# A Nyström attention and gated feed-forward kernel: every stage cut into one step per engine, w_out read by fours, and a new written order of 1,091 steps

## The chip, the cores and the metric

The kernel runs on one core of a Trainium2 chip. A core has five engines that run side by side and meet at semaphores: TensorE (PE in the profile; its weight loads are shown apart as PEld), VectorE (DVE), ScalarE (ACT), GpSimd (POOL) and SyncE (SP, which here only issues DMAs). Each engine works through its own instructions strictly in the order in which the program wrote them. The metric is the device time of one execution in microseconds.

## The reference, cut to what matters

Eight batches of eight heads, 576 tokens, 64 numbers per head. Each head goes through a Nyström attention with 32 landmarks (means of 18 tokens), and the result through a feed-forward block without a nonlinearity but with a product in the middle.

```python
q_lm = q.reshape(B, H, 32, 18, D).mean(axis=3)      # and k_lm alike
A  = softmax(q    @ k_lm.T / 8)                     # 576 x 32
Bm = softmax(q_lm @ k_lm.T / 8)                     # 32 x 32
C  = softmax(q_lm @ k.T    / 8)                     # 32 x 576
Z  = Bm.T / (norm1(Bm) * norminf(Bm) + 1e-6)
for _ in range(6):
    Z = 2 * Z - Z @ Bm @ Z                          # inverse of Bm, by iteration
x  = (A @ Z @ C @ v)                                # 8 x 8 x 576 x 64 -> 4608 x 512
out = (((x @ w1) * (x @ w2)) @ w3) @ w_out          # 512 -> 1024 -> 1024 -> 512
```

## The kernel before

**The fold.** As nothing stands between `w3` and `w_out`, the kernel first forms `w34 = w3 @ w_out` once (1024 x 512). Both factors are split into a high and a low fp16 part, and three products are added up (`product`, L526 to L533: 8 row blocks j of 8 chunks c of 3 matmuls of 512 columns, 192 matmuls). TensorE needs `w3` transposed: 64 fp32 transposes of 128x128 through the identity, four to a PSUM tile (`turn` in `fold`, L514 to L523), and ScalarE and VectorE then cut that tile into its two parts (L522, L523). `split` (L508) does the same for `w_out`. Twelve matmuls on zeros (L599) come ahead of it.

**The attention of one batch.** `turn` (L140) transposes q and k in 32x32 blocks on VectorE; `landmarks` adds up the groups of 18 (on GpSimd for all batches but the first); `scores_b`, `norms`, `squares` and six steps of `inverse` (L388) make the inverse of the 32x32 matrices, for two batches at a time in `CHAINS`; `scores_c`, `scores_a`, `values`, `denominators`, `normalise`, `landmark_values` do the rest. Their matmuls use 32-row or 64-row tiles of the array. Landmark queries and keys lie in a tile `lm` in which neighbouring landmarks stand 16 bytes apart (`lmk`, L234), and this view is the stationary operand of L274 and L322, and both operands of L248.

**The feed-forward.** `project` (L430) makes w1 and w2 as the landmarks see them (four parts G0 to G3 per batch), `up` (L451) the two products of 576 tokens for one of eight blocks of 128 features (ScalarE copies the first, L459; VectorE multiplies it with the second, L461), and `down` (L470) the 36 output tiles of 128 tokens: eight matmuls of 512 columns, a copy on ScalarE (L499), two DMAs from SyncE (L502).

**Memory that sets waits.** PSUM has three tiles `big`, one `small`, one `acc` (L89 to L97). `acc` is that of `product` and of `down`. SBUF holds three rows of `w3`, six of `w_out`, four turned halves of `w3`, and q and k of two batches.

**What sets the order.** A string `ORDER` (L32) of words, one for each stage: `U3a.2` is the first half of `up` for block 3 of batch 2, `W0.14` the first half of output tile 14, `F` the next piece of the fold, `TK`, `TQ` the block transposes of k and q, `SK`, `SQ` their landmark sums, `LK`, `LQ`, `LV` the loads. The loop at L656 calls the stage, which writes all of its instructions, for all engines, at that place. So two stages can't be interleaved on one engine in another order than on the others.

Of the kernel before, what the change touches and what calls it, by code (L numbers as in the profile page):

```python
# [29 lines left out]
CHAINS = ((0,), (1, 2), (3, 4), (5, 6), (7,))  # L30

ORDER = """  # L32
F F F F F F F F F F F F F TK0.0 F F F F F TQ0.0 TQ1.0 F F L3.3 F TK1.0 F F F F F SK0.0 SK1.0 F F
SQ0.0 P.4 F F F F L3.5 F L3.7 F F TQ0.1 TK0.1 SQ1.0 F F L3.6 TK1.1 F E.0 F B.0 F C0.0 SK0.1 N.0
F F F A0.0 R.0 FV.0 TQ1.1 F SK1.1 F I0.0 F F D.0 I1.0 F I2.0 Y0.0 Y1.0 SQ0.1 Y2.0 LK0.2 F X.0 F
I3.0 LK1.2 F F F I4.0 V0.0 V1.0 SQ1.1 LQ0.2 LQ1.2 E.1 F LK0.3 TK0.2 TK1.2 F LK1.3 I5.0 F V2.0
LV0.2 F TQ0.2 TQ1.2 A0.1 Z.0 SK0.2 LV0.1 LV1.1 F M0.0 LV2.1 F LV3.1 D.1 Y0.1 Y1.1 Y2.1 G0.0 G1.0
G2.0 M1.0 SK1.2 F SQ0.2 TK0.3 G3.0 TK1.3 C0.1 X.1 F F F F U0a.0 U0b.0 U1a.0 U1b.0 U2a.0 U2b.0
LQ0.3 TQ0.3 LQ1.3 LK0.4 U3a.0 LV1.2 V0.1 U3b.0 SQ1.2 E.2 U4a.0 U4b.0 B.1 U5a.0 U5b.0 N.1 V1.1
SK0.3 V2.1 R.1 U6a.0 U6b.0 TQ1.3 U7a.0 I0.1 M0.1 LK1.4 LQ0.4 U7b.0 W0.0 SK1.3 I1.1 W1.0 I2.1  # L40
A0.2 LV2.2 TK0.4 LV3.2 W0.1 I3.1 TK1.4 W1.1 I4.1 M1.1 LQ1.4 W0.2 TQ0.4 I5.1 W1.2 SQ0.3 SQ1.3
TQ1.4 Z.1 SK0.4 E.3 SK1.4 SQ0.4 LV0.3 C0.2 G0.1 D.2 G1.1 G2.1 W0.3 Y0.2 G3.1 V0.2 V1.2 Y1.2 V2.2
LV0.4 Y2.2 U0a.1 U0b.1 LV1.3 LK0.5 U1a.1 U1b.1 LV1.4 LK1.5 X.2 U2a.1 U2b.1 U3a.1 U3b.1 Z.2 SQ1.4
E.4 U4a.1 U4b.1 U5a.1 G0.2 TK0.5 U5b.1 U6a.1 U6b.1 M0.2 LQ0.5 LQ1.5 W1.3 U7a.1 LV2.3 U7b.1 LV3.3
M1.2 W0.4 G1.2 G2.2 G3.2 B.3 TK1.5 W1.4 U0a.2 A0.3 W0.5 U0b.2 U1a.2 LV2.4 D.3 Y0.3 Y1.3 SK0.5
U1b.2 Y2.3 C0.3 W1.5 LK0.6 U2a.2 U2b.2 U3a.2 W0.6 X.3 U3b.2 U4a.2 N.3 SK1.5 V0.3 V1.3 V2.3 R.3
U4b.2 TK0.6 W1.6 LV3.4 U5a.2 U5b.2 W0.7 TQ0.5 U6a.2 I0.3 M0.3 LK1.6 TQ1.5 W1.7 I1.3 SQ0.5 LQ0.6
U6b.2 W0.8 I2.3 W1.8 I3.3 U7a.2 U7b.2 W0.9 I4.3 M1.3 W1.9 I5.3 A0.4 LQ1.6 Z.3 C0.4 W0.10 G0.3
G1.3 G2.3 D.4 W1.10 Y0.4 LV0.5 SQ1.5 G3.3 E.5 LV1.5 U0a.3 U0b.3 Y1.4 W0.11 TK1.6 Y2.4 U1a.3
U1b.3 U2a.3 U2b.3 LK0.7 X.4 TK0.7 W1.11 TQ0.6 U3a.3 U3b.3 U4a.3 V0.4 V1.4 V2.4 SK0.6 SK1.6 A0.5  # L50
TQ1.6 W0.12 U4b.3 LV2.5 U5a.3 LV3.5 LK1.7 SQ0.6 U5b.3 Z.4 U6a.3 U6b.3 LV0.6 LV1.6 U7a.3 U7b.3
W1.12 M0.4 M1.4 G0.4 W0.13 SQ1.6 E.6 TK1.7 G1.4 G2.4 G3.4 SK0.7 W1.13 D.5 Y0.5 LQ0.7 Y1.5 Y2.5
C0.5 U0a.4 X.5 W0.14 SK1.7 W1.14 U0b.4 U1a.4 U1b.4 B.5 V0.5 V1.5 V2.5 U2a.4 U2b.4 N.5 W0.15
U3a.4 U3b.4 W1.15 A0.6 TQ0.7 R.5 M0.5 W0.16 U4a.4 I0.5 U4b.4 U5a.4 I1.5 U5b.4 U6a.4 I2.5 LV0.7
LQ1.7 TQ1.7 SQ0.7 SQ1.7 W1.16 I3.5 U6b.4 U7a.4 I4.5 M1.5 U7b.4 I5.5 LV2.6 LV1.7 LV3.6 W0.17 Z.5
C0.6 E.7 W1.17 D.6 G0.5 G1.5 G2.5 W0.18 Y0.6 Y1.6 G3.5 Y2.6 U0a.5 U0b.5 X.6 W1.18 U1a.5 U1b.5
U2a.5 B.7 V0.6 V1.6 V2.6 U2b.5 U3a.5 N.7 U3b.5 W0.19 U4a.5 U4b.5 U5a.5 U5b.5 Z.6 U6a.5 W1.19
LV2.7 G0.6 G1.6 G2.6 LV3.7 R.7 W0.20 A0.7 I0.7 W1.20 U6b.5 M0.6 M1.6 W0.21 U7a.5 G3.6 D.7 I1.7
U7b.5 W1.21 U0a.6 U0b.6 Y0.7 U1a.6 Y1.7 U1b.6 W0.22 W1.22 C0.7 U2a.6 W0.23 U2b.6 U3a.6 Y2.7
U3b.6 W1.23 V0.7 V1.7 V2.7 X.7 I2.7 U4a.6 W0.24 U4b.6 I3.7 U5a.6 W1.24 I4.7 U5b.6 U6a.6 I5.7  # L60
W0.25 Z.7 U6b.6 W1.25 M0.7 M1.7 G0.7 W0.26 U7a.6 U7b.6 W1.26 G1.7 G2.7 G3.7 W0.27 U0a.7 U0b.7
W1.27 U1a.7 U1b.7 W0.28 U2a.7 U2b.7 W1.28 U3a.7 U3b.7 U4a.7 W0.29 W1.29 U4b.7 U5a.7 U5b.7 W0.30
U6a.7 U6b.7 U7a.7 W1.30 U7b.7 W0.31 W1.31 W0.32 W1.32 W0.33 W1.33 W0.34 W1.34 W0.35 W1.35
# [4 lines left out]
def kernel(  # L68
# [93 lines left out]
    def constants():  # L162

        mask4 = consts.tile([128, 4, 32], FP32, name="mask4")
        eye = consts.tile([128, 2, 32], FP32, name="eye")
        onesq = consts.tile([128, 2, 4, 2, 4], FP16, name="onesq")
        nc.vector.memset(mask4, 0.0)
        nc.vector.memset(onesq, 0.0)
        for h in range(4):
            sl = slice(32 * h, 32 * h + 32)  # L170
            nc.vector.memset(mask4[sl, h, :], 1.0)
            for qd in range(2):
                nc.vector.tensor_copy(out=eye[sl, qd, :], in_=ident[sl, sl])
                nc.vector.memset(onesq[sl, qd, :, qd, h:h + 1], 1.0 / X64)

        selc = consts.tile([128, 2, 4, 128], FP16, name="selc")
        lomask = consts.tile([128, 1], FP32, name="lomask")
        selr = consts.tile([128, 8], FP32, name="selr")
        nc.vector.memset(selc, 0.0)
        nc.vector.tensor_tensor(out=selr, in0=eye[:, 0, 0:8], in1=eye[:, 0, 8:16], op=ALU.add)  # L180
        nc.vector.reduce_sum(out=lomask, in_=eye[:, 0, 8:16], axis=AX.X)
        nc.vector.tensor_scalar(out=lomask, in0=lomask, scalar1=-1.0, scalar2=None, op0=ALU.mult)
        for c in range(4):
            sl = slice(32 * c, 32 * c + 32)
            for qd in range(2):
                nc.vector.tensor_copy(
                    out=selc[sl, qd, c, :].rearrange("p (h m) -> p h m", m=32),
                    in_=selr[sl, 4 * qd:4 * qd + 4].unsqueeze(2).to_broadcast([32, 4, 32]),
                )
        eye2 = consts.tile([128, 32], FP32, name="eye2")  # L190
        nc.vector.tensor_tensor(out=eye2, in0=eye[:, 0], in1=eye[:, 0], op=ALU.add)
        bt = consts.tile([128, 4, 64], FP32, name="bt")
        for i in range(4):
            nc.vector.tensor_copy(out=bt[:, i, 32:64], in_=eye[:, 0])
        xsp = [consts.tile([128, 256], FP32, name=f"xsp{i}") for i in range(2)]
        for t in xsp:
            nc.vector.memset(t, 0.0)
        return mask4, eye, eye2, onesq, selc, lomask, bt, xsp


# [18 lines left out]
    def exchange(st):  # L219
        if st["b"] < 2:  # L220
            psE = big()
            for x in range(2):
                nc.tensor.matmul(psE[:, 0, 256 * x:256 * x + 256], pick[:, x, :],
                                 st["lm"][:, :, x].rearrange("p t l c e -> p t (l c e)"),
                                 start=True, stop=True)
            nc.scalar.copy(out=st["lm"].rearrange("p t x l c e -> p x t (l c e)"),
                           in_=psE[:, 0, :].rearrange("p (x t f) -> p x t f", x=2, t=2))
            return
# [104 lines left out]
    def values(st, n):  # L333
        if n == 0:
            st["psV"] = big()
# [169 lines left out]
    def fold(pf, wof, w3f, wsp, warm_up):  # L505
# [39 lines left out]
        for n, (j, c) in enumerate(order):  # L545
            for f, *args in before.get(n, ()):
                f(*args)
# [158 lines left out]
```

## Time and profile before

| | |
|---|---|
| time, median of 3 runs | 264.17 us (264.1 to 264.42) |
| span of the profiled execution | 261.8 us |
| PE busy | 251.5 us, 96% of the span |
| DVE, ACT, POOL busy | 173.8, 134.7, 103.2 us |
| granted TensorE clock, mean | 0.999 |
| DMA | 37.78 MB, mean 144 GB/s |

No time is given for the profiled execution as a whole; its span, from the first to the last instruction of the program, is 2.4 us below the median of the runs. A line of the groups is read so: line of the code, engine, operation, what it writes and reads, partitions x elements, how many; then busy time, the mean in ns of one, and the idle time of its engine just before them.

### The profile page before, as it was taken

The page shows a single profiled execution, that of the slowest core. Times are in us where ns is not written, and L with a number is a line of the kernel's source. Part 1 is how long each engine was busy: PE and PEld are TensorE (multiplying, and loading weights), DVE is VectorE, ACT ScalarE, POOL GpSimd, SP SyncE. Part 2 cuts the span into 40 slices and gives each one's busy share as a digit, 9 for nine tenths or more (in the row PEclk, how much of TensorE's full clock was granted, in tenths as well). Part 3 has the DMA queues.
Part 4 walks back from the last instruction along what each step waited for, and adds up shares of the span by engine and source line. Part 5 has one row for each costly group of instructions (what it writes and reads, how often), then busy time and mean ns, then how long its engine had stood idle before and what let it go on. Part 6 is the DMA issues. An engine that isn't in the chain of part 4 may idle for free.

```text
span 261.8 us, 10518 instructions
## 1 busy us (share of the span) xinstructions
PE 251.5 (96%) x4578; PEld 148.7 (57%) x4578; DVE 173.8 (66%) x352; ACT 134.7 (51%) x305; POOL 103.2 (39%) x134
## 2 busy tenths in 40 slices
PE   7999999998989999999999999999999999999993
PEld 3455554454556558557654674766476556656642
DVE  8765887556958687788856958767775656464410
ACT  4543236343652565576449546746646555455531
POOL 3630018998981999027092597504400000000000
PEclk9999999999999999999999999999999999999999
DMA  6999998999963448976668496933640713222355
GB/s 236 333 243 284 245 248 191 183 137 240 175 105 50 120 101 167 216 195 114 131 100 162 101 214 150 161 58 86 147 86 3 173 43 80 45 62 61 81 118 127
DMA packets 25070, 37.78 MB, mean 144 GB/s; under 512 B 4672, under 2 KB 13120, under 8 KB 25024
## 3 DMA queue, kind: packets, MB, share of 16 engines
q1 hardware_dynamic: 14704, 24.65, 36.9%
q0 software_dynamic: 9728, 11.54, 28.1%
q10 hardware_dynamic: 592, 0.92, 1.1%
q8 instruction: 36, 0.59, 1.0%
q14 instruction: 10, 0.08, 0.1%
HBM read 38.80 MB, written 9.44 MB: 184 GB/s over the span
## 4 chain that ended last, share of the span: by engine, by line
PE 89%; DVE 4%; ACT 3%; issue 1%; DMA 1%; SPq 0%; DVEq 0%; ACTq 0%
PE big L455 23%; PE acc L495 22%; PE acc L530 14%; PE big L442 5%; PE big L344 5%; PE big L399 4%; PE big L517 2%; PE small L530 2%; PE big L382 2%; PE small L421 2%; PE big L274 1%; PE big L495 1%; PE big L322 1%; DVE ab L461 1%; PE small L248 1%
## 5 line engine op out<-in xcount | busy, mean ns | idle before, releaser
L455 PE MATMUL big<-ahat,gt 128*128 128x288 f16 x512 | 73.1, 287 | 0.7 <-DVE ab L461 0.6
L495 PE MATMUL acc<-w,ab 128*128 128x512 f16 x264 | 67.2, 380 | 0.0
L461 DVE TENSOR_TENSOR ab<-a_sb,big 128x576 f16<-128x576 f16 x64 | 48.0, 750 | 27.2 <-ACT a_sb L459 16.8
L455 PEld LDWEIGHTS <-gt 128*128 128x128 f16 x512 | 48.3, 98 | 21.1 <-issue 3.1
L459 ACT CAST a_sb<-big 128x576 f16<-128x576 f32 x64 | 40.8, 640 | 33.9 <-PE big L455 32.9
L206 POOL TENSOR_TENSOR tr<-qkT 128x1024 f32<-128x1024 f16 x14 | 29.7, 2123 | 70.0 <-DVE qkT L143 69.8
L530 PE MATMUL acc<-wsp,w3t 128*128 128x512 f16 x168 | 41.3, 380 | 0.7 <-ACT w L533 0.5
L495 PEld LDWEIGHTS <-ab 128*128 128x128 f16 x280 | 25.3, 98 | 24.9 <-issue 3.5
L499 ACT ACTIVATE o_sb<-acc 128x512 f32<-128x512 f32 x33 | 19.8, 599 | 19.5 <-PE acc L495 19.1
L530 PEld LDWEIGHTS <-w3t 128*128 128x128 f16 x192 | 18.1, 98 | 18.9 <-issue 1.3
L143 DVE STREAM_TRANSPOSE qkT<-qkn 128x576 uint32<-128x576 uint32 x32 | 24.0, 763 | 2.0 <-DMA qkn<-in_k_dram 2.0
L448 DVE TENSOR_SCALAR gt<-big 128x1024 f16<-128x1024 f32 x16 | 19.1, 1211 | 3.1 <-PE big L442 3.0
L446 ACT ACTIVATE gt<-big 128x1024 f16<-128x1024 f32 x16 | 15.9, 1032 | 5.9 <-PE big L442 5.9
L211 POOL TENSOR_TENSOR tr<-tr 128x512 f32<-128x512 f32 x14 | 17.9, 1282 | 0.6
L442 PE MATMUL big<-wup,zt 64*32 64x512 f16 x512 | 17.4, 380 | 0.2 <-ACT en L282 0.2
L523 DVE SCALAR_TENSOR_TENSOR w3t<-big,w3t 128x512 f16<-128x512 f32 x16 | 11.0, 687 | 10.0 <-ACT w3t L522 10.0
L522 ACT ACTIVATE w3t<-big 128x512 f16<-128x512 f32 x16 | 9.5, 596 | 13.9 <-PE big L517 13.8
L284 DVE STREAM_TRANSPOSE ent<-en 128x576 f32<-128x576 f32 x16 | 12.1, 768 | 4.4 <-ACT en L282 4.4
L344 PE MATMUL big<-vt,ent 64*32 64x64 f32 x1152 | 14.2, 226 | 0.0
L282 ACT ACTIVATE en<-big 128x288 f32<-128x288 f32 x32 | 12.7, 411 | 2.9 <-PE big L274 2.7
L344 PEld LDWEIGHTS big<-vt,ent 64*32 64x32 f32 x1152 | 12.7, 105 | 2.0 <-ACT a_sb L459 0.5
L328 ACT ACTIVATE eat<-big 128x576 f16<-128x576 f32 x16 | 9.6, 652 | 7.3 <-PE big L322 7.3
(214 smaller groups left out, 285.2 us busy)
## 6 DMA issues: line engine op xcount, KB each, us to landing
out_dram<-o_sb SPq DMA_DIRECT2D x70, 128.0 KB, 2.5
vt<-in_v_dram SPq DMA_DIRECT2D x16, 288.0 KB, 5.3
vt<-in_v_dram SPq DMA_DIRECT2D x32, 144.0 KB, 4.0
qkn<-in_k_dram POOLq DMA_DIRECT2D x12, 288.0 KB, 5.4
qkn<-in_q_dram POOLq DMA_DIRECT2D x12, 288.0 KB, 4.9
w3f<-in_moe_w_dram SPq DMA_DIRECT2D x6, 512.0 KB, 6.7
wup<-in_moe_w_dram POOLq DMA_DIRECT2D x4, 512.0 KB, 25.3
wof<-in_moe_w_out_dram SPq DMA_DIRECT2D x6, 256.0 KB, 4.5
```

The lines of the kernel that those rows point to most:

```text
L143: nc.vector.transpose(out=st["qkT"][:, t, prs].rearrange("p c r q e -> p (c r q e)").bitcast(U32), in_=st["qkn"][:, t, prs, :].rearrange(" ...
L206: add(out=tr, in0=x[:, :, 0:4, :], in1=x[:, :, 4:8, :], op=ALU.add)
L211: add(out=tr[:, :, 0:2, :], in0=tr[:, :, 0:2, :], in1=tr[:, :, 2:4, :], op=ALU.add)
L344: nc.tensor.matmul(psV[32 * o:32 * o + 32, qd, 0:64], ent[sl, pr, r, :], vt[sl, pr, 64 * r:64 * r + 64], start=(r == 0), stop=(r == RT - 1 ...
L442: nc.tensor.matmul(psG[o:o + 32, qd, :], zt[rs, i, h, :], wup[rs, h, w, fs], start=(i == 0), stop=(i == 1), tile_position=(64 * qd, o))
L448: nc.vector.tensor_scalar(out=g[:, :, w, fs], in0=psG, scalar1=1.0 / ZS, scalar2=None, op0=ALU.mult)
L455: nc.tensor.matmul(p[:, c, 0:HS], st["g"][:, qd, w, 128 * j:128 * j + 128], st["ahat", qd][:, c, :], start=(qd == 0), stop=(qd == 1))
L459: nc.scalar.copy(out=st["a_sb"], in_=p[:, :, 0:HS])
L461: nc.vector.tensor_tensor(out=st["ab"][:, j, st["t0"]:st["t0"] + S].rearrange("p (c s) -> p c s", c=2), in0=st["a_sb"], in1=p[:, :, 0:HS], ...
L495: nc.tensor.matmul(pso[:, :], ab[:, j, t0:t0 + 128], w34[:, j, :], start=(j == 0), stop=(j == 7))
L499: nc.scalar.activation(out=o_sb, in_=pso, func=AXF.Copy, scale=1.0 / (X64 * X64))
L530: nc.tensor.matmul(psW[j][:, :], turned[j, c // 4][:, a, c % 4, :], wsp[:, b, c, :], start=(c == 0 and a + b == 0), stop=(c == 7 and a == 1))
```

## The change

All stages become generators that yield after what they have for one engine. The order has a word for each such part: `U3.2` appears four times (matmuls, copy, matmuls, product), `W.14` four times (half the matmuls, the other half, copy, DMAs), `I2.3` three times (matmuls, VectorE, ScalarE), and so on; the parts of different stages can be woven in any way that keeps each stage's own order. Written out in parts, the old order has 1,091 as well, and the instructions are the same in number, but for what follows.

- `fold` is gone; `split`, `turned_w3` and `product` are steps of the order, as are the loads of q, k, w1 and w2 at the start, the single warm-up matmuls and eleven pieces of the constants on VectorE.
- The rows of `w_out` are read by fours: chunk c of half x holds rows 512x + 4m + c on partition m, where it was rows 128c + m. To fit, the transposes take every fourth column of a row of `w3`, that is fp32 numbers 16 bytes apart, where they were neighbours. `NPE = 8` makes all of the transposes TensorE's: the branch with a block transpose on VectorE, and the loads cut in eight, are there for j of 8 and more, and there are none.
- The GpSimd copy that holds back the load of row block 4 writes four numbers per partition instead of one.

```diff
-F F F F F F F F F F F F F TK0.0 F F F F F TQ0.0 TQ1.0 F F L3.3 F TK1.0 F F F F F SK0.0 SK1.0 F F
-SQ0.0 P.4 F F F F L3.5 F L3.7 F F TQ0.1 TK0.1 SQ1.0 F F L3.6 TK1.1 F E.0 F B.0 F C0.0 SK0.1 N.0
...
-U3a.4 U3b.4 W1.15 A0.6 TQ0.7 R.5 M0.5 W0.16 U4a.4 I0.5 U4b.4 U5a.4 I1.5 U5b.4 U6a.4 I2.5 LV0.7
-LQ1.7 TQ1.7 SQ0.7 SQ1.7 W1.16 I3.5 U6b.4 U7a.4 I4.5 M1.5 U7b.4 I5.5 LV2.6 LV1.7 LV3.6 W0.17 Z.5
-C0.6 E.7 W1.17 D.6 G0.5 G1.5 G2.5 W0.18 Y0.6 Y1.6 G3.5 Y2.6 U0a.5 U0b.5 X.6 W1.18 U1a.5 U1b.5
...
+NPE = 8
...
+K S.0 K K K K T0.0 K T0.0 K L.2 K S.0 T0.0 S.1 K S.1 K K K T0.1 T0.1 S.2 S.3 LK1.2 KC T0.1 F.0 S.4
+F.0 F.1 S.2 LO.7 KC F.1 LO.6 T1.0 KC F.0 S.3 F.1 L.3 KC T1.0 KC LF F.0 T1.0 F.1 TK1.2 S.5 T1.1 KC
+T1.1 T1.2 S.4 S.5 F.0 S.7 S.6 F.0 T1.1 T0.2 S.6 T1.2 F.1 T0.2 F.0 S.7 T0.3 F.0 F.1 F.0 T0.2 T1.3
+T1.2 LF F.2 F.2 KC TK0.0 F.2 LQ0.2 T1.3 F.2 F.2 F.2 TK1.0 TQ0.0 T1.3 F.2 LK0.2 F.1 P.4 P.4 KC T0.4
...
+R.5 U4.4 LV2.6 U0.4 U4.4 U6.4 U0.4 U4.4 W.15 I0.5 W.16 U6.4 I0.5 I0.5 M0.5 U4.4 I1.5 I1.5 U5.4 LV1.7
+I1.5 TK1.7 I2.5 I2.5 U5.4 W.16 I2.5 I3.5 U7.4 LV3.6 M0.5 I3.5 I3.5 I4.5 I4.5 W.16 SK0.7 I4.5 U6.4
+U6.4 U7.4 I5.5 I5.5 I5.5 W.17 U7.4 U7.4 Z.5 Z.5 C.6 W.17 SK1.7 Z.5 C.6 U5.4 C.6 E.7 U5.4 G0.5 D.6
+C.6 G3.5 W.16 G0.5 W.17 LV2.7 G2.5 G2.5 G3.5 G1.5 G1.5 D.6 W.18 LV1.6 U4.5 U4.5 U0.5 W.17 U0.5 U4.5
...
-        eng.dma_start(out=wof[c], in_=moe_w_out[128 * c:128 * c + 128, :])
+        eng.dma_start(out=wof[c], in_=moe_w_out.rearrange("(x m c) o -> x c m o", x=2, c=4)[c // 4, c % 4])
...
-                nc.tensor.transpose(out=pst[:, 0, 128 * c4:128 * c4 + 128],
-                                    in_=w3f[j][:, 512 * cc + 128 * c4:512 * cc + 128 * c4 + 128],
-                                    identity=ident[:, :])
...
+    def turned_w3(j, cc):
+        if j < NPE:
+            wt = big()[:, 0, :]
+            src = w3f[j].rearrange("p (x m c) -> p x c m", x=2, c=4)
+            for c in range(4):
+                nc.tensor.transpose(out=wt[:, 128 * c:128 * c + 128], in_=src[:, cc, c], identity=ident[:, :])
...
+        yield
+        w3t = w3ts[j, cc] = pf.tile([128, 2, 4, 128], FP16, name="w3t", bufs=4)
+        hi, lo = (w3t[:, i].rearrange("p c j -> p (c j)") for i in range(2))
+        nc.scalar.activation(out=hi, in_=wt, func=AXF.Copy, scale=WS)
+        yield
+        nc.vector.scalar_tensor_tensor(out=lo, in0=wt, scalar=WS, in1=hi,
+                                       op0=ALU.mult, op1=ALU.subtract)
...
-    def up(st, j, w):
...
+    def up(st, j):
+        for w in range(2):
+            p = big()
...
+            yield
+            if w == 0:
+                a_sb = po.tile([128, 2, HS], FP16, name="a_sb", bufs=2)
+                nc.scalar.copy(out=a_sb, in_=p[:, :, 0:HS])
+                yield
...
-        nc.gpsimd.tensor_copy(out=w3f[j][:, 0:1], in_=sts[0]["qkn"][:, 1, 0, 0:1])
+        nc.gpsimd.tensor_copy(out=w3f[j][:, 0:DF:DF // 4],
+                              in_=sts[0]["qkn"][:, 1, 0, 0:1].to_broadcast([128, 4]))
...
+    pab, live = [], {}
     for word in ORDER.split():
...
+        if live[word] is not None:
+            next(live[word], None)
```

In the new order k and q of batch 2 are loaded before those of batch 1 (`LK1.2` ahead of the six steps `LF`, which load k and q of batches 0 and 1 and then w1 and w2), and w1 and w2 after those.

## The prediction

> **What bounds the kernel now.** I read the page first, its busy times and the chain.
>
> ```profile
> PE 251.5 (96%) x4578; PEld 148.7 (57%) x4578; DVE 173.8 (66%) x352; ACT 134.7 (51%) x305; POOL 103.2 (39%) x134
> ...
> PE 89%; DVE 4%; ACT 3%; issue 1%; DMA 1%; SPq 0%; DVEq 0%; ACTq 0%
> ```
>
> TensorE carries 89% of the chain, so a change to the order can win only TensorE's waits. The table of stretches tells how much that is. Its columns are stretch and length, then busy time and instructions of PE, PEld, DVE, ACT and POOL, the granted clock, DMA share and GB/s.
>
> ```profile
> 50.00:60.00 10.00, 8.73 (x240) 5.04 (x237) 4.94 (x11) 3.40 (x8) 9.09 (x12) 1.00 1.01 160
> 70.00:80.00 10.00, 8.41 (x196) 6.12 (x194) 7.09 (x14) 5.05 (x15) 7.79 (x10) 1.00 0.69 107
> 110.00:120.00 10.00, 10.00 (x194) 5.42 (x193) 8.78 (x15) 6.83 (x23) 4.03 (x3) 1.00 0.77 173
> ```
>
> Over all stretches from 6.5 to 250 us PE is idle for 4.6 us: 1.3 in 50 to 60, 1.6 in 70 to 80, 0.5 from 20 to 40, 0.4 from 80 to 100, and from 110 on only 0.3. The waits by engine, for PE, say what ended the larger ones.
>
> ```profile
> PE big L349 <- issue: 1.3, 1, 1.3
> ...
> PE small L290 <- DVE bm L260: 1.0, 1, 1.0
> PE big L455 <- DVE ab L461: 0.6, 2, 0.4
> PE acc L530 <- ACT w L533: 0.5, 2, 0.2
> ```
>
> The 1.3 us of "issue" wait for nothing that a new order promises to mend. So about 3.3 us are to be won from idle time, all of it before 110 us; the second half of the kernel can only lose.
>
> The groups of like instructions, shapes apart, give the price of the transposes that the change alters, and of loads of weights and matmuls with and without a step of 16 bytes:
>
> ```profile
> L517 PE MATMUL big<-ident,w3f 128*128 128x128 f32 x64 | 10.0, 280 | 0.3 <-DMA w3f<-in_moe_w_dram 0.3
> L442 PEld LDWEIGHTS <-zt 64*32 64x32 f16 x512 | 6.0, 91 | 8.7 <-issue 4.1 <-ACT a_sb L459 0.7 <-ACT zt L426 0.2
> L248 PE MATMUL small<-lm 32*32 32x32 f16 x128 | 2.9, 231 | 0.0
> L322 PEld LDWEIGHTS <-lm 32*32 32x32 f16 x256 | 2.5, 134 | 1.9 <-issue 1.9
> L305 PEld LDWEIGHTS small<-bt 32*32 32x32 f32 x128 | 2.1, 105 | 0.8 <-issue 0.4 <-DVE csT L293 0.2
> L399 PE MATMUL big<-sz__1620,tz__1618 32*32 32x32 f32 x32 | 0.4, 197 | 0.0
> ```
>
> And the chain in order of time (start, us, what) shows what a step costs with its neighbours.
>
> ```profile
> 52.36 0.44 PE big L517 x4
> ...
> 85.07 0.38 PE big L399 x32
> 85.45 0.97 PE acc L495 x4
> 86.42 0.38 PE big L399 x32
> ...
> 215.55 0.86 PE acc L495 x4
> ```
>
> Four transposes take 0.44 us (0.11 each). Half an output tile takes 0.86 us, but 0.97 ahead of a step on 32-row tiles: going from the whole array to small tiles costs 0.11.
>
> **The change, part by part.** The sum is made against the profiled span of 261.8 us; the runs' median is 2.4 us above it, and I add the same difference to both.
>
> *Transposes that read every fourth number.* 64 transposes, now with numbers 16 bytes apart. No row has fp32 at that step, but `lm` has fp16 at exactly 16 bytes: a load of 32 such columns takes 134 ns (L322), where 32 fp32 columns side by side take 105 (L305) and 32 fp16 columns 91 (L442). As a moving operand 32 such columns take 231 ns (L248) against 197 for fp32 side by side (L399). So whichever operand is meant, the step costs: 29/32 = 0.9 ns a column from the fp32 load, 34/32 = 1.1 from the matmul, 43/32 = 1.3 from the fp16 load. For 128 columns that is 116, 136 and 172 ns more than 110. The bounds are 0 (the load hidden behind the matmul before it) and 172. I take 116, by the fp32 row, the nearest in type. Eight transposes (row blocks 0 and 1, first halves) lie ahead of 8.9 us, where TensorE waits for VectorE anyway; if that cover is gone, they cost 0.9. The other 56 lie between matmuls of the fold, where PE was busy: 56 x 0.116 = **+6.5** (0 to +9.6).
>
> [...]
>
> *Head.* The constants held VectorE from 0.9 to 6.5 us; the first product came at 6.9 and the first of row block 1 at 8.9. Now the constants are spread out, and w_out's low parts come first. But the second low part of w3 stands behind `KC` (0.7: two memsets and the first masks), so that I add up 6.8 for the first, 7.5 for w_out's second, 8.2, 8.9: the product of row block 1 begins when it did. Then VectorE has three more `KC`, `TK1.2` (0.77) and a fifth ahead of w_out's chunk 4: by the same addition it is ready at 14.9, and PE would be there at 13.6. The 12 transposes between cover 12 x 0.116 = 1.4 of it: **0** (without that cover +0.5 against before, which had waits of its own there).
>
> *Queues.* `LK1.2` goes on GpSimd's queue ahead of the copy that holds back the q and k loads. 288 KB at that queue's price (28.1% of 16 engines for 11.54 MB, so 6.4 us of all engines a MB) is 1.8 us taken from the first loads. The ones pushed back are w_out's chunks 2 to 5 (landed at 7.2 to 8.9) and w3's second halves (8.2, 9.5), used at 9.5 or later: 0, at most +1.8. On SP, row block 2 of w3 moves ahead of the last two w_out chunks, which wait for their buffers: 0, since these landed at 10.9 and 12.3 and are used at about 16. Row blocks 4 and 6 are issued when k of batch 0 has landed (17.6 before) and took 6.4 and 7.6 us to land, so about 25 and 27; PE gets there at 20.7 + 5 + the longer transposes, 27: 0, at most +1. w1 and w2, now behind k and q of three batches, landed at 42.8 and are used at 63.7; with 2.4 MB more ahead, at the 7.5 us a MB at which that queue ran from 9.5 to 42.8, they land at 60: 0. Output DMAs as steps of their own free SP from waiting for copies; no PE wait in the list hangs on SP, 0. Four numbers in the GpSimd copy instead of one: 193 ns (L624) for 183 (L619), 0. w_out by fours: 2 KB a partition as before, 0 to +1.
>
> *Waits that go.* In the fold a row block's copy to `w34` held `acc` twice (0.5); now a transpose or a product of block 1 stands between: **-0.5**. In 70 to 80 us PE waited 1.6, the most of it for `bm` after 24 matmuls; `B.1` and `N.1` now have nine PE steps between them. But by the mean durations VectorE has 11.7 us of work from `G3.0` to `R.1` and PE 11.2, so `big` will still be late by some tenths at a time: **-1.0** (0 to -1.6).
>
> *Switches.* Counted along the written orders, steps on small tiles follow whole-array steps 57 times instead of 65, and are followed by them as often: 8 x (0.11 + 0.09), where 0.09 is what the same chain gives for the way back (a part of `project` takes 0.56 ahead of a whole-array step and 0.47 otherwise): **-1.6** (0 to -1.6).
>
> *Waits that come.* A step of the inverse follows the one before it after VectorE's and ScalarE's parts (292 and 372 ns): from the first's end at 85.4 to the next start at 86.3, 0.92. Before, 0.8 or more of other work lay between. In the new order of batches 5 and 6, `I1`, `I3` and `I4` are followed by one half of `up` only (0.49 + 0.09): 3 x 0.34 = **+1.0** (0 to +1.0). Behind `C.6` stand `G0.5 G3.5 G2.5 G1.5` with three `big` tiles; ScalarE (two exponentials of 1.24, then 1.03) and VectorE (0.77, then 1.21 twice) free them later than PE asks: **+0.6** (0 to +1.5).
>
> Sum: 6.5 - 0.5 - 1.0 - 1.6 + 1.0 + 0.6 = +5.0, a span of 266.8, and 264.2 + 5.0 = **269.2 us**.
>
> **The rivals.**
> *The step costs nothing* (ends on the other side). If the transposes stay at 0.11, the sum is -1.5, and the head's 0.5 is uncovered: -1.0, 263.2. For it: PEld is busy for 57% only and runs beside PE. Against it: four transposes take 0.44 while each of their loads takes 144 ns, so the loads already stand in the pace. It decides at 1.5/56 = 27 ns a transpose. [...]
> *The step costs more*: 172 ns by the fp16 row, 9.6 in all: 272.3.
> *w2 comes late*: if its queue ran at 8.9 us a MB instead of 7.5, w2 would land at 70 and PE would just wait (`G1.0` comes after 56.2 us of PE work; `U0.0`, after 61.7 us of it, started at 69.7, so 8.0 of waits, and 6.5 of longer transposes: 70.7); each us a MB beyond adds 7. I put +3: 272.2. Against it: a reserve of 10 us.
> *The order does what it can and the step is free*: none of the waits that come, -3.1: 261.1.
>
> **How the numbers follow.** Forecast 0.53, step dearer 0.17, w2 late 0.05, step free 0.17, order alone 0.08. 0.2% (0.5 us) is about what runs of this kernel can tell from no change. Slower is 0.53 + 0.17 + 0.05 = 0.75; the free step at 263.2 lies near that bound, so 0.03 of its 0.17 goes to "same", and faster is 0.22. The range from 262.5 to 274 leaves out the order alone and a dearer step with the bounds of the other terms. The likeliest case by itself spans 267 to 271.5.
>
> **What would show it.** The transposes' line: start to start 0.22 to 0.28 where it was 0.11, loads of 230 ns and more, PE's idle time about the same. `U0.0` (69.7 before) starts at 75 to 76. The waits for `bm` and for `w` are gone, and L399 waits for `sz_` about 170 us. The forecast is wrong if the transposes' loads stay near 144 ns, or if `U0.0` starts before 71.

## The result and the profile after

The changed kernel takes 286.44 us (median of 4 runs, 285.11 to 287.14), the kernel before 264.3 beside it: a ratio of 1.082 (95% interval 1.077 to 1.087), 22 us slower. The prediction had the direction, 269.2 us, and a range that ended at 274. The profiled execution has a span of 283.3 us, 21.5 more than before. Times here are medians of a kernel's runs within 1.5% of its fastest, as the ratios are; where that leaves runs out, the median of all follows in brackets.

The page of the changed kernel, lines of its parts 1 to 4 (busy time of each engine, granted clock in 40 slices, the queue that brings instructions, the chain):

```profile
PE 257.3 (91%) x4578; PEld 153.0 (54%) x4578; DVE 173.1 (61%) x352; ACT 132.6 (47%) x305; POOL 103.2 (36%) x134
...
PEclk9999999989995999999999979999999999999998
...
q8 instruction: 36, 0.59, 0.9%
...
PE 69%; DMA 15%; issue 6%; DVE 5%; SPq 3%; ACT 1%; POOL 0%; ACTq 0%; POOLq 0%
```

TensorE's share of the chain fell from 89% to 69%. DMA took 15% of it and "issue" 6%, where each had 1%. Nearly all of the DMA part lies ahead of 54 us, in loads of `w_out` and of k (the last of them from 38.1 to 53.8 us). The clock has dips that it did not have. The table of stretches says where (columns as in the prediction):

```profile
50.00:60.00 10.00, 6.62 (x78) 3.09 (x76) 4.78 (x11) 2.32 (x7) 9.41 (x13) 0.83 1.17 209
70.00:80.00 10.00, 10.00 (x175) 5.71 (x152) 8.07 (x12) 5.82 (x15) 6.92 (x9) 1.00 0.40 90
80.00:90.00 10.00, 6.26 (x184) 4.77 (x183) 4.14 (x12) 3.05 (x12) 9.37 (x12) 0.82 0.96 172
110.00:120.00 10.00, 9.04 (x112) 6.82 (x118) 7.75 (x15) 5.80 (x11) 1.34 (x3) 1.00 0.75 159
160.00:170.00 10.00, 7.27 (x202) 4.53 (x201) 5.21 (x10) 1.69 (x4) 5.53 (x6) 0.83 0.57 158
```

The stretch from 70 to 80 is full, as hoped. Four others now hold 3.4, 3.7, 1.0 and 2.7 us of idle TensorE, and in three of them the clock fell to 0.82 or 0.83. The waits of TensorE name the causes:

```profile
PE big L337 <- issue: 8.5, 3, 3.7
PE big L396 <- ACT sz__694 L409: 3.4, 1, 3.4
PE big L396 <- issue: 2.0, 1, 2.0
PE big L527 <- DMA w3f<-in_moe_w_dram: 1.4, 1, 1.4
PE big L460 <- issue: 1.4, 2, 0.9
...
PE acc L544 <- DVE wsp L519: 1.1, 1, 1.1
PE small L282 <- DVE bm L247: 0.7, 1, 0.7
PE big L396 <- ACT sz__3850 L409: 0.3, 1, 0.3
```

All of TensorE's waits in this view add up to 21.2 us, before to 5.8. "Issue", a wait that nothing in the profile releases, is 8.5 + 2.0 + 1.4 = 11.9 of it, where it was 1.3. Three of these waits stand in the middle of `values` (L337), as the timeline (start, duration, what, idle time before) shows for the largest:

```profile
82.27 0.93 PE L337 MATMUL big<-vt,ent 64*32 64x64 f32 x71
86.95 0.53 PE L337 MATMUL big<-vt,ent 64*32 64x64 f32 x17 [3.74 <-issue]
...
88.16 2.13 PE L460 MATMUL big<-ahat,gt 128*128 128x288 f16 x8
```

One stage stops for 3.7 us between two of its own matmuls, with the same operands ready; behind the wait, eight matmuls of `up` take 2.13 us at a granted clock of 0.50, where eight took 1.14 from 182.8 us at 1.00.

**A theory.** Queue q8 brings instructions: 36 packets of 16 KB in either kernel, and TensorE has some 9,200 records (4578 matmuls, as many weight loads and some 45 waits for semaphores), so 256 to a packet. I counted how many of these had begun when an "issue" wait set in:

| kernel | waits set in at (us) | begun by then | remainder by 256 |
|---|---|---|---|
| before | 58.4 | 1217 | 193 |
| after | 83.0, 111.8, 139.8, 162.3, 216.7, 242.5 | 1985, 3265, 4289, 5313, 7617, 8641 | 193 each time |

And while TensorE waited, or just before, a packet of q8 was on its way. So theory F: TensorE has one block of 256 instructions ahead and no more. When it passes the end of a block the next is asked for; in these two traces 51 of the 72 packets start within 2 us behind that, 7 ahead of it and 14 later (at the latest 4.1), they take 0.9 to 1.8, and TensorE goes on 1.2 to 1.6 us after the end of the one it waited for. A block whose 256 instructions pass in less than all that, some 3.5 us as I estimate it from these numbers, ends in a wait. `values` has 320 instructions in 1.6 us (from 186.2 us in the changed kernel). In the changed kernel the blocks that ended in waits had passed in 1.3 to 3.4 us; in the kernel before, the shortest without one took 3.84 (from 84.5 us), and the one with one 4.2, its packet 3.4 late. Seven packets of these two traces started over 3 us after TensorE had gone on into the next block, all of them while the DMA engines were at a share of 1.0 to 1.2; whether that is what held them back was not tested. The rivals: the neighbourhoods of the new order, the load of v, and the transposes of the prediction.

### The profile page after: what moved, and what is told of

Same layout as the page of the kernel before. It is cut to its first block, busy times and chain, and to the rows that moved or that the text cites. A ratio compares the mean times of both kernels' runs of the same rounds, so it can differ in the third digit from the quotient of the medians.

```text
span 283.3 us, 10482 instructions
## 1 busy us (share of the span) xinstructions
PE 257.3 (91%) x4578; PEld 153.0 (54%) x4578; DVE 173.1 (61%) x352; ACT 132.6 (47%) x305; POOL 103.2 (36%) x134
## 4 chain that ended last, share of the span: by engine, by line
PE 69%; DMA 15%; issue 6%; DVE 5%; SPq 3%; ACT 1%; POOL 0%; ACTq 0%; POOLq 0%
PE big L460 23%; PE acc L502 19%; DMA qkn<-in_k_dram 12%; PE big L445 6%; PE big L337 5%; PE acc L544 4%; PE big L396 4%; DMA wof<-in_moe_w_out_dram 3%; SPq L512 2%; PE big L378 2%; PE small L422 1%; PE big L261 1%; PE big L316 1%; PE small L298 1%; DVE gt L452 1%
## 5 line engine op out<-in xcount | busy, mean ns | idle before, releaser
L460 PE MATMUL big<-ahat,gt 128*128 128x288 f16 x512 | 74.5, 291 | 1.7 <-issue 1.4
L502 PE MATMUL acc<-w,ab 128*128 128x512 f16 x264 | 68.0, 383 | 0.1
L465 ACT CAST a_sb<-big 128x576 f16<-128x576 f32 x64 | 39.9, 641 | 47.8 <-PE big L460 28.9
L460 PEld LDWEIGHTS <-gt 128*128 128x128 f16 x512 | 49.5, 100 | 22.9 <-issue 3.8
L544 PEld LDWEIGHTS <-w3t 128*128 128x128 f16 x192 | 18.8, 100 | 20.7 <-issue 2.8
L337 PE MATMUL big<-vt,ent 64*32 64x64 f32 x1152 | 14.6, 228 | 8.5 <-issue 8.5
L450 ACT ACTIVATE gt<-big 128x1024 f16<-128x1024 f32 x16 | 15.9, 1025 | 6.5 <-PE big L445 6.5
L337 PEld LDWEIGHTS big<-vt,ent 64*32 64x32 f32 x1152 | 12.8, 106 | 10.2 <-issue 9.0
L445 PE MATMUL big<-wup,zt 64*32 64x512 f16 x512 | 18.0, 387 | 0.0
L130 POOL DMA_DIRECT2D qkn<-in_q_dram x14 | 10.2, 733 | 12.4 <-DVE qkT L166 9.3
L382 DVE TENSOR_TENSOR ahat<-eat,big 128x576 f16<-128x576 f16 x16 | 11.8, 748 | 3.4 <-PE big L378 3.4
```

What stands on the lines that cost most here:

```text
L337: nc.tensor.matmul(psV[32 * o:32 * o + 32, qd, 0:64], ent[sl, pr, r, :], vt[sl, pr, 64 * r:64 * r + 64], start=(r == 0), stop=(r == RT - 1 ...
L445: nc.tensor.matmul(psG[o:o + 32, qd, :], zt[rs, i, h, :], wup[rs, h, w, fs], start=(i == 0), stop=(i == 1), tile_position=(64 * qd, o))
L460: nc.tensor.matmul(p[:, c, 0:HS], st["g"][:, qd, w, 128 * j:128 * j + 128], st["ahat", qd][:, c, :], start=(qd == 0), stop=(qd == 1))
L465: nc.scalar.copy(out=a_sb, in_=p[:, :, 0:HS])
L502: nc.tensor.matmul(pso[:, :], ab[:, j, t0:t0 + 128], w34[:, j, :], start=(j == 0), stop=(j == 7))
L544: nc.tensor.matmul(psW, w3ts[j, c // 4][:, a, c % 4, :], wsp[:, b, c, :], start=(c == 0 and a + b == 0), stop=(c == 7 and a == 1))
```

## Experiments

**The order before, its blocks shifted by 120 instructions.**

```diff
-    warm_up(7)
+    warm_up(3)
+    for i in range(64):
+        sl = slice(32 * (i % 4), 32 * (i % 4) + 32)
+        nc.tensor.matmul(psw[sl, 0, 0:32], warm[sl, 0:32], warm[sl, 0:32], start=True, stop=True,
+                         tile_position=(sl.start, sl.start))
```

> The kernel before with its order untouched. Four of the wide warm-up matmuls at the start give way to 64 tiny ones (32x32, 32 columns, on zeros), so that TensorE's stream holds 120 instructions more ahead of all real work; the work and the result are the same. **Theory F (fetch):** TensorE's instructions arrive in blocks of 256, and only one block ahead; a block of which the 256 instructions pass in less than about 3.5 us makes TensorE wait for the next. In the trace of before the ends of the blocks lie so that no block but one passes in under 3.9 us. Moved by 120, eight blocks do (at about 56, 80, 99, 127, 157, 176, 204 and 232 us, each within the 64-row matmuls of `values`), and the sum of what they lack of 3.6 us is 15.6: 277 to 285 us, with 'issue' waits of 1 to 3 us at these places. **Rival (the order):** the waits without a releaser belong to steps that stand beside each other in the new order or to a load; nothing of that is touched here, so 264 to 265 us and 'issue' waits of 1.3 in all, as before.

Measured: 288.6 us, ratio 1.086 (1.079 to 1.094). The old order, shifted, is as slow as the new one. TensorE's waits in this kernel:

```profile
PE big L344 <- issue: 4.6, 3, 1.8
PE small L305 <- issue: 4.4, 2, 2.2
PE big L399 <- issue: 4.0, 2, 2.6
PE big L322 <- issue: 2.9, 1, 2.9
```

15.9 us of "issue"; all eight waits set in with the remainder 193 (1217, 2241, 3265, 4289, 5569, 6337, 7617, 8641). The sum of what the blocks lacked, 15.6, was right; the rest of the 24 is clock (0.967) and some 1.7 us at the head, where four wide warm-ups fewer left TensorE idle before its first transposes.

**The control, 256 instructions more.** One wide warm-up fewer, 129 tiny matmuls.

> The control: the kernel before, its order untouched, with one wide warm-up matmul fewer and 129 tiny ones more, that is 256 instructions of TensorE more ahead of the work. **Theory F (fetch, blocks of 256):** the ends of the blocks fall on the same work as in the kernel before, so the waits go again: 264 to 266.5 us, 'issue' waits of 1 to 2 us in all. **Rival (the tiny matmuls themselves, or any longer stream, cost the time that the shift by 120 showed):** at least the 288 us of that run.

Measured: 264.68 us, ratio 1.002 (0.999 to 1.005). A whole block more costs nothing that the runs show; the waits are those of before:

```profile
PE big L349 <- issue: 1.3, 1, 1.3
...
PE small L290 <- DVE bm L260: 1.0, 1, 1.0
```

Besides them only a wait of 0.9 us in the fold is new. So neither the tiny matmuls nor the longer stream made the loss of the first run, but where the blocks end. This decides for theory F against the neighbours, which are the same in all three kernels.

**The dose, 48 instructions more.** Seven warm-ups, 24 tiny matmuls.

> The kernel before with 24 tiny matmuls more after its seven warm-up matmuls: 48 instructions. **Theory F (fetch):** the sum of what the blocks lack of 3.6 us is 8.0 here, where it was 15.6 for a shift by 120, which cost 24 us; so about +11, 272 to 280 us, with the largest waits about 98 (2.2 us), 199 (2.3) and 155 us (1.0). **Rival (the blocks have another length, or there is slack for more than one of them):** 264 to 266, or as much as the shift by 120.

Measured: 277.37 us, ratio 1.047 (1.041 to 1.052), 10.8 us of "issue", the largest 2.5 us at 100.8, 2.3 at 179.3 and 1.7 at 207.8. The size was forecast from the blocks' durations alone (11 us more, measured 13); the wait at 179.3 was not among those named.

**The changed kernel, shifted by 104.** The same loop with 52 tiny matmuls behind the first five warm-ups.

> The changed kernel with 52 tiny matmuls on zeros (104 instructions of TensorE) after its first five warm-up matmuls, where TensorE waits for w3. **Theory F (fetch):** the waits without a releaser change place. Those at 83 and 162 us (inside `V.1` and `V.3`) go, and 2 to 3.5 us each come at about 62, 107, 184 and 213, with 1 to 3 left at 138 to 142 and at 242. Their sum by the blocks' durations is 13.4 against 9.3 for the changed kernel as it is: 288 to 296 us. **Rival (the order or the load of v):** the waits stay inside the same four steps, at 83, 140, 162 and 242 (plus the cost of the tiny matmuls, under 1): 286 to 287.5 us.

Measured: 289.5 us (289.85), ratio 1.092 (1.086 to 1.099), 15.7 us of "issue". That time alone hardly parts it from the changed kernel (1.077 to 1.087); the places of the waits do. The wait at 162 went; new ones stand at 63.3, 110.2, 185.4 and 215.1, and two are left at 144.6 and 245.7, as forecast. The one at 83 moved to 89.0, into `R.1`, which I had not forecast. All have the remainder 193.

**The fours undone.**

```diff
-        eng.dma_start(out=wof[c], in_=moe_w_out.rearrange("(x m c) o -> x c m o", x=2, c=4)[c // 4, c % 4])
+        eng.dma_start(out=wof[c], in_=moe_w_out[128 * c:128 * c + 128, :])
...
-            src = w3f[j].rearrange("p (x m c) -> p x c m", x=2, c=4)
+            src = w3f[j].rearrange("p (x c m) -> p x c m", x=2, c=4)
```

> The changed kernel with w_out read by rows of 128c + m again, and the transposes taking columns that are neighbours; order and steps as changed. **As predicted (the step of 16 bytes costs 0.116 a transpose):** 6.5 us less, 279 to 281 us. **Rival (the trace of after: start to start 120 ns in the middle where it was 109, so 11 ns for each of 56):** 0.6 us less, 285 to 287 us, and the loads' mean back from 206 to about 144 ns.

Measured: 284.96 us, ratio 1.077 (1.071 to 1.083), which overlaps the interval of the changed kernel: 1.5 us less, and not 6.5. The loads of the transposes, in the groups of the changed kernel and then of this one:

```profile
L527 PE MATMUL big<-ident,w3f 128*128 128x128 f32 x64 | 10.9, 301 | 1.6 <-DMA w3f<-in_moe_w_dram 1.4
L527 PEld LDWEIGHTS big<-ident,w3f 128*128 128x128 f32 x64 | 9.6, 206 | 4.1 <-issue 2.6
```

```profile
L527 PEld LDWEIGHTS big<-ident,w3f 128*128 128x128 f32 x64 | 8.4, 156 | 4.7 <-issue 3.0
```

The step of 16 bytes makes a load 50 ns longer (206 against 156), but the median from start to start only 11 (120 against 109), 0.7 us for 64. In the trace of the changed kernel such loads start 0.12 us apart and last 0.21 each (from 14.9 us), so that they overlap, and most of the longer load does not show in the pace. Nor does the time of the kernel show it: 1.071 to 1.083 here, 1.077 to 1.087 in the changed kernel.

**The turns of k of batch 3 later.** `TK0.3` and `TK1.3` go behind VectorE's part of `I4.0`.

```diff
-... LV3.1 F.5 F.5 TK0.3 A.0 I0.0 I0.0 ... I1.0 I2.0 TK1.3 I2.0 F.6 ... V.0 I4.0 E.1 F.6 D.0 I4.0 V.0 E.1
+... LV3.1 F.5 F.5 A.0 I0.0 I0.0 ... I1.0 I2.0 I2.0 F.6 ... V.0 I4.0 E.1 F.6 D.0 I4.0 TK0.3 TK1.3 V.0 E.1
```

> The changed kernel with the two turns of k of batch 3 on VectorE (`TK0.3`, `TK1.3`) moved behind the fifth inverse step of batch 0, so that VectorE no longer waits for that load between two inverse steps. **Theory W (the late load of k of batch 3 holds VectorE, and so the inverse, and so TensorE):** the wait of 3.4 us at 51.4 goes, and with it the half clock from 55 to 59; -4 to -5 us, 281 to 283 us. **Rival (TensorE would wait there for its next block of instructions or for w3 anyway, or makes the gain up later by a wait for the next block):** -1.5 or less, 285 to 287 us.

Measured: 283.3 us (285.4), ratio 1.076 (1.066 to 1.085), an interval that overlaps that of the changed kernel; two runs took 283.3 us and two 287.5. In the profiled run, one of 287.5, the wait of 3.4 for `sz_` is gone from the list and others have come:

```profile
PE big L396 <- issue: 3.5, 2, 1.9
...
PE big L207 <- POOL lm L200: 0.7, 1, 0.7
```

A block's end at 61 us now costs 1.5, and `E.1` waits for GpSimd's landmark sums; "issue" is 14.2 us in all, where it was 11.9. So the late load makes the wait for `sz_`; whether mending it wins 3 us or nothing, this run does not decide.

**More to do, and faster.** 176 instructions that do nothing, in two places of the changed kernel.

```diff
+PAD = {(0, 1): 64, (3, 1): 24}
...
     def up(st, j):
         for w in range(2):
             p = big()
+            for i in range(PAD.get((st["b"], j), 0) if w == 0 else 0):
+                sl = slice(32 * (i % 4), 32 * (i % 4) + 32)
+                nc.tensor.matmul(p[sl, 0, 0:32], st["g"][sl, 0, 0, 0:32], st["ahat", 0][sl, 0, 0:32],
+                                 start=True, stop=True, tile_position=(sl.start, sl.start))
```

> The changed kernel with its order untouched and 176 instructions of TensorE more, which do nothing for the result: 64 tiny matmuls ahead of the first half of `U1.0` and 24 ahead of that of `U1.3` (into PSUM that the real matmul then starts anew). By the trace after they move the ends of the blocks so that what the blocks lack of 3.6 us falls from 8.4 us in sum to 0.9, left in one inverse step of batch 3; they cost 1.0 themselves. **Theory F (fetch):** the waits without a releaser at 83, 112, 140, 162 and 242 go, and with them the half clock behind them: -8 to -13, 274 to 279 us, from a kernel with more to do. **Rival (V's neighbours, the load of v):** 287 to 288 us.

Measured: 273.65 us (276.01), ratio 1.036 (1.031 to 1.042): 12.8 us less than the changed kernel (10.4 by the median of all runs), from nothing but where its blocks end. TensorE's waits in the profiled run of 277.2 us:

```profile
PE small L299 <- issue: 2.4, 1, 2.4
PE big L397 <- ACT sz__694 L410: 2.4, 1, 2.4
...
PE big L397 <- issue: 1.5, 2, 1.0
...
PE big L461 <- issue: 1.1, 1, 1.1
```

"Issue" fell from 11.9 to 5.7 and not to the 0.9 that I had reckoned. By this kernel's own trace five blocks still end in waits, having passed in 1.7 to 3.6 us; they lack 3.9 us of 3.6 in sum. The largest, 2.4 in `R.1`, ends a block of 3.2 us whose packet started 3.4 us late.

**An order evened out on TensorE.** Two orders made from the changed one so that every block should take 3.8 us.

```diff
-U3.0 C.1 U4.0 LK1.4 B.1 LV1.2 U6.0 U6.0 V.1 F.7 V.1 U3.0 V.1 LV0.2 B.1 N.1 V.1 ...
+U3.0 C.1 LK1.4 B.1 V.1 V.1 U4.0 U6.0 U4.0 LV1.2 U3.0 U6.0 F.7 U3.0 U6.0 U7.0 U7.0 V.1 LV0.2 B.1 N.1 LQ0.4 V.1 ...
```

> The changed kernel with its order evened out on TensorE: of its 443 steps 59 stand more than two places from where they were and 27 more than three (by the most, halves of `up`, of output tiles and thirds of `values`), chosen by nothing but the instructions and the duration of each, so that 256 instructions in a row take at least 3.8 us wherever a block ends; by the durations of the trace after, the blocks lack 0.6 us of that in sum, where the changed kernel lacks 11.0. Same work, same instructions, fours and head as in the change. **Theory F (fetch):** the waits without a releaser at 83, 112, 140, 162 and 242 go, and the stretches at a clock of 0.82 to 0.84 behind them: -11 to -14, 272 to 276 us; the waits for the load of k and those of the head stay. **Rival (the new neighbours themselves cost the time, or the moved steps wait for VectorE and ScalarE instead):** 280 us or more.

> A second order made in the same way from the changed one by other moves (68 steps more than two places away): the blocks lack 1.1 us in sum, and TensorE goes 98 times between whole-array and small-tile steps, where the first goes 108 and the changed kernel 114 times. **Theory F (fetch):** 272 to 276 us, as the first, and no more than 1.5 us apart from it. **Rival (it is not the blocks but which stages are neighbours):** the two differ by 3 us or more.

Measured: 314.91 us (ratio 1.190, 1.187 to 1.193) and 311.34 (1.177, 1.175 to 1.180): 25 to 28 us worse than the changed kernel, a plain miss. In the first one's list the blocks are mended, and everything else is not:

```profile
PE acc L501 <- ACT o_sb L507: 3.8, 5, 2.2
PE big L459 <- DVE ab L466: 2.2, 4, 1.3
PE big L395 <- DVE tz__2427 L304: 2.2, 1, 2.2
...
PE big L336 <- issue: 0.6, 1, 0.6
PE big L315 <- issue: 0.6, 1, 0.6
```

"Issue" is 1.2 us in all, and none in the second, as theory F said of these waits. It was wrong on the time: both rivals hold, the second with 3.6 us between the two orders. The other waits rose from 9.3 to 38.9 us in the first: the moved halves of `up`, output tiles and inverse steps now come before VectorE and ScalarE have freed their PSUM or made their operands. Two orders that were good for the fetch alone took 311 to 315 us. The same with the turns of k later:

> The evened order with the two turns of k of batch 3 behind the fifth inverse step of batch 0 as well. **If the load's wait and the blocks' waits are separate causes:** the -4 that the move promised and did not bring alone comes now, since no block's end gives it back: 268 to 272 us. **Rival (VectorE, which then has the turns to do later, takes it back whatever the blocks do):** within 1.5 us of the evened order without the move.

Measured: 312.4 us in a single run (317.66), so that a small gain can't be told from none; the forecast is missed by 40 us.

**What is the rest?** The kernel with the 176 instructions is still 10 us slower than the kernel before. All that follows stands on the kernel with the 176 instructions. First the turns of k again:

> The same 176 instructions, and the two turns of k of batch 3 behind the fifth inverse step of batch 0. **If the load's wait is a cause of its own, which the blocks' ends gave back in part when the turns alone were moved (a wait of 1.7 us at a block's end came at 61):** 3 to 4.5 us less than with the 176 instructions alone, 270 to 275 us. **Rival (VectorE takes it back):** within 1.5 us of it.

Measured: 275.55 us, ratio 1.043 (1.040 to 1.046): no gain. The wait for `sz_` is replaced by one for the sums of batch 1 from 57.5 to 60.4 us:

```profile
PE big L208 <- POOL lm L201: 2.9, 1, 2.9
```

These sums are late because their load is: q of batch 1 lands at 45.3 us in the changed kernel, at 31.0 before. `LK1.2` gives one of the two buffers of q and k to batch 2, so batch 1 is issued only when batch 0 has been turned (26.1 us instead of 11.9). So I put head and loads back.

```diff
 a_pad_kc:
-K S.0 K K K K T0.0 K T0.0 K L.2 K S.0 T0.0 S.1 K S.1 K K K T0.1 T0.1 S.2 S.3 LK1.2 KC ...
+KC KC KC KC KC KC KC KC KC KC K S.0 K K K K T0.0 K T0.0 K T0.1 L.2 K S.0 T0.0 S.1 K S.1 K K K T0.1 ...
 a_pad_loads (a_pad_both has both):
-... LK1.2 ... TK1.2 ... LF F.2 F.2 KC TK0.0 F.2 LQ0.2 ... LK0.2 ... TQ1.0 ... LQ1.2 TK0.2 FV.0 LF ... LF ...
+... LF LF LF LF LF F.2 F.2 KC TK0.0 ... TQ1.0 LK0.2 LK1.2 LQ0.2 LQ1.2 ... FV.0 ... TQ1.1 LK0.3 LK1.3 ...
```

> The kernel with the 176 instructions, and the head put back in part: ten of the eleven pieces of the constants run on VectorE before anything else, as in the kernel before (it waits there until 5.7 us), and the first transposes of row block 1 come ahead of five warm-up matmuls that stood before them. **Theory H (the head):** the first products come at about 7 to 8 us instead of 8.8, the wait of 0.9 to 1.2 at 16 for a low part of w_out goes: -1.5 to -2.5 against the kernel with the 176 instructions, 273.5 to 274.5 us. **Rival (w_out's later landing, not VectorE, sets the head, or the loads take the gain back):** within 0.8 us of it.

> The kernel with the 176 instructions, and the loads on GpSimd's queue in the order of the kernel before: k and q of batches 0 and 1, w1, w2, then batch 2 (behind batch 0's turns), then batch 3; the turns of batches 2 and 3 on VectorE moved behind them accordingly. TensorE's order is untouched. **Theory L (k of batch 2 first takes one of two buffers, so that batch 1 is loaded only after batch 0 is turned, and everything on VectorE and GpSimd behind it is late):** q of batch 1 lands at about 31 us instead of 45, the waits for `bm` at 46 and for `sz_` at 51 go and none takes their place at 57, and the clock stays up: -4 to -6, 270 to 272 us. **Rival (VectorE or GpSimd is behind there for other reasons):** within 1.5 us of 276.

> Both edits at once. **If head and loads are separate causes:** the sum, -5.5 to -8.5: 267.5 to 270.5 us, so that 3 to 6 us over the kernel before are left for the order's own waits (the inverse steps of batches 5 and 6 with 1.45, the waits left at blocks' ends with 3 to 5, the 176 instructions with 1). **Rival (one wait behind both):** no better than the better of the two.

Measured: 276.15 (ratio 1.044, 1.038 to 1.049), 282.96 (1.069, 1.062 to 1.076) and 282.74 us (1.068, 1.060 to 1.076). The head was not put back by my edit: five warm-ups of 0.43 us each, twice the 0.21 that a matmul of 512 columns takes later, still stood ahead of the first product, which came at 9.7 us. So this run tells nothing of the head. With the loads put back q of batch 1 lands at 32.2, and the waits for `bm` and `sz_` are gone, but my loads of batch 2 held GpSimd until 42.5 us, and behind them the copy that releases v and, on SyncE, the last block of w3:

```profile
PE big L531 <- DMA w3f<-in_moe_w_dram: 10.5, 2, 9.1
```

Two more tries moved these loads later:

> As the run with the loads put back, but the loads of batches 2 and 3 stand behind GpSimd's copy for v and behind the load of the last row block of w3, as in the kernel before (there they were issued at 47 us). **Theory L (loads):** q of batch 1 lands at about 31, nothing of w3 is late, no wait over 1 us between 40 and 60: 270 to 272.5 us, -4 to -6 against the kernel with the 176 instructions. **Rival (the early loads were as good; something else holds VectorE and GpSimd there):** 275 to 277 us.

Measured: 276.55 us, ratio 1.046 (1.043 to 1.049). One wait of over 2 us is left before 75 us, again for the sums of batch 1, since GpSimd stood for w1 and w2 ahead of them:

```profile
PE big L208 <- POOL lm L201: 4.3, 1, 4.3
```

> The kernel with the 176 instructions, with the loads in the order of the kernel before and, on GpSimd, those of batch 2 behind the first landmark sums of batch 1, those of batch 3 behind the last; turns on VectorE accordingly (batch 2 after the fifth inverse step of batch 0, batch 3 ahead of `G3.0` and behind `TQ0.3`). TensorE's order is that of the change. **Theory L (loads and GpSimd's order):** no wait over 1 us between 10 and 75 us, the clock stays up there: -4.5 to -6.5 against the kernel with the 176 instructions, 269.5 to 271.5 us. **Rival (there is always one more wait behind: TensorE's new order asks for batch 1 too early):** 274 us or more.

Measured: 276.51 us, ratio 1.047 (1.045 to 1.049). That wait is gone too; a block's end takes 2.0 at 59, and `B.1` waits for the exchange of batch 2:

```profile
PE small L234 <- DMA lm<-lm: 4.5, 4, 2.0
PE big L397 <- issue: 2.8, 2, 2.0
```

None of the repairs of the early part, each of the wait on top, gained anything; each time the next one showed. The last did work where it was made: the first `up` starts at 71.6 us, where it started at 75.0 with the 176 instructions and at 69.5 in the kernel before. Behind it the waits of `B.1`, 4.5 us in all from 75 to 81 us, took the gain back. The loads are late in the change, that is shown; what they cost in the end is not.

**A better kernel.** The old order with theory F and the list of its own waits in hand:

```diff
-... LK1.3 I5.0 F V2.0 ... X.1 F F F F U0a.0 ... U5b.0 N.1 V1.1 SK0.3 V2.1 R.1 U6a.0 U6b.0
+... LK1.3 I5.0 F F F V2.0 ... X.1 F F U0a.0 ... U5b.0 V1.1 SK0.3 V2.1 N.1 U6a.0 R.1 U6b.0
```

> The kernel before with two edits of its order, which leave the blocks' ends within 12 instructions of where they were. Two pieces of the fold move ahead of `V2.0`, so that the block that passed in 4.2 us (54.2 to 58.4, its fetch late by 3.4) takes 5.5; and `N.1` goes behind `V2.1`, since it waited 1.1 us for `bm` with nothing in its place, with a half of `up` between it and `R.1`. **Theory F:** the wait of 1.3 us at 58.4 goes, and the one for `bm`: -2.4, 261.5 to 262.5 us. **Rival (VectorE sets the pace there, and TensorE waits for it a little later):** 263.5 to 264.5.

Measured: 263.26 us, ratio 0.9956 (0.994 to 0.997): 1.0 us faster than the kernel before, less than half of what theory F gave and a little better than the rival, and the fastest of all that ran. The two large waits are gone, and smaller ones came:

```profile
PE big L344 <- issue: 0.7, 1, 0.7
PE big L455 <- DVE gt L448: 0.5, 1, 0.5
```

> The kernel before with the two pieces of the fold ahead of `V2.0` alone. **Theory F:** the wait of 1.3 us at 58.4 goes; if VectorE's copies of `g` then hold TensorE at 68 for 0.5, as with both edits, 0.8 is left: 263.3 to 263.6 us, and the edit of `N.1` added little. **Rival (the gain of both edits was that of `N.1`):** 264.0 to 264.5 us.

Measured: 264.02 us, ratio 0.999 (0.997 to 1.001): no difference. The 1.3 us of "issue" are gone here as well, but TensorE then waits for VectorE's copy of `g` and for the landing of w3. The gain of both edits needed that of `N.1`, as the rival said.

## Why the prediction was wrong

**The step that failed** is a sentence before the sum: "The 1.3 us of 'issue' wait for nothing that a new order promises to mend." It took them for a constant. By the runs they are set by how the written order of TensorE lies over blocks of 256 instructions (15.9 us of them after a shift by 120, 1.3 after one by 256), which a rewritten order shifts. They became 11.9; taking a good half of them away again, without touching the order, made the kernel 12.8 us faster. No rival of the prediction had it.

The direction came out right for another reason than the one forecast: the +6.5 for the transposes, which alone made the sum positive, was 0.7. Of the 21.5 us by which the profiled execution is longer, 5.9 lie ahead of the first `up` and 15.6 behind it. Behind it the ends of blocks take 11.9 and the half clock (below) 5.1, which together is more than the 15.6.

Point by point:

- *Transposes, +6.5:* 0.7 by the pace, and 1.5 by the run, whose interval overlaps that of the change. A longer load was real (50 ns of the 116), but I laid it into the pace because "four transposes take 0.44 while each of their loads takes 144 ns". Loads overlap (0.21 us each, 0.12 apart), and of the 50 ns 11 came into the pace (120 against 109). The prediction's own sign, loads over 230 ns and 0.22 from start to start, did not come. The rival "the step costs nothing" was right about this term and wrong about the end.
- *Head, 0:* first product at 8.8 us instead of 6.9. Five warm-ups ahead of the first transposes instead of seven leave TensorE idle for 1.4 us; the next ones take 0.42 us each until 7.9 and 0.21 from there (the granted clock reads 1.00 in both stretches, and the trace's own clock records begin at 7.9). The wait for w_out's chunk 4, which I had seen and called covered by longer transposes, is there with 1.1: the cover was the term above. What the head is worth in the end stays open.
- *Queues, 0:* q of batch 1 14 us later, since a load moved forward takes a buffer. I had counted bytes and places in the queue, and not buffers. The wait for `sz_`, 3.4, came of it; put right, it moved to other waits, so its net worth is not settled. The rival of a late w2 did not come: the last part landed at 61.6 us (forecast 60) and was used at 69.4 or later.
- *Waits that go:* right. There is none for `w` in the list, nor for `bm` at 78 us, and 70 to 80 us is full (10.00 busy against 8.41), though by then the work is some 6 us behind. The 0.7 for `bm` in the list is another wait, at 46.6 us for batch 0.
- *Waits that come:* the inverse steps of batches 5 and 6 wait 3 x 0.3, forecast 1.0. Behind `C.6` nothing came, forecast 0.6.
- *Switches, -1.6:* no run isolates them.
- *Not in the sum at all:* the clock. In the changed kernel the granted clock is 0.50 for 3.4 us from 55.7, 6.8 us from 86.4 and 3.4 us from 164.9, each time begun within 0.7 us of the end of a wait of 2.7 to 3.7 us; the kernel before has no such stretch until its last matmul is done (0.50 from 261.1 us). At half clock these 13.7 us hold, by reckoning, the work of 6.8. None followed the waits of 2.0 us and less. So these three long waits were paid for again.
- *The sign `U0.0` at 75 to 76* came (75.4), for another reason: by then the kernel had lost 5.9 us to the head, `bm`, `sz_`, the half clock and 0.7 of longer transposes. A sign that several causes can give decides nothing. Neither of the two signs of being wrong came: the loads took 206 ns, not 144, and `U0.0` did not start before 71.

What stays open: the profiled execution with the 176 instructions is 13.6 us longer than that of the kernel before. 8.2 of it lie behind the first `up`: blocks' ends are 5.3 there, where before had none, a stretch at half clock of 3.4 us costs 1.7, the inverse 0.9, the 176 themselves by reckoning 1.0. The 5.5 ahead of it are shared by head, early loads and another such stretch, and the runs did not part them.

## What to carry to other kernels

A wait without a releaser in the middle of one stage is a reason to count instructions: see whether its index leaves the same remainder by 256 each time (193 here). A reordering, or even a few instructions more at the head, could then cost or win 10 to 24 us here on one engine without any of its dependencies changing; compare orders at several shifts before the difference is put down to the order. And an engine's order may not be evened out for one resource without the others (the two evened orders took 25 to 28 us more): the waits at the top of a list are replaced by the next ones.

## What the runs showed of the hardware

- TensorE mostly stood still at the end of a block of 256 instructions that had passed in under 3.5 us: in the twenty traces of this case all 79 of its waits that nothing released, of 0.2 to 3.7 us, set in with the remainder 193. Of the 70 blocks that passed in under 3.5 us, 64 ended in such a wait; 15 longer ones, of 3.6 to 5.0 us, did too. That agrees with one block ahead; the fetch itself shows only in the 36 packets of q8, of 16 KB each.
- 120 instructions more at the head made the old order 24 us slower, 256 made it 0.4 us slower with an interval that includes none, and 176 inside the new order made it 12.8 us faster.
- Tiny matmuls of 32x32 and 32 columns on four tiles in turn took 0.69 us for 64, so a shift costs little time to test.
- fp32 loads of 128 columns 16 bytes apart took 206 ns against 156 side by side, and cost 11 ns each in the pace.
